# Loading K of a batch row in one transfer with 32 KB runs in an attention decode kernel

## The chip, the cores and the metric

The kernel runs on one core of one Trainium2 chip. The core has TensorE (PE: matrix multiplies and transposes, reading SBUF and writing PSUM), VectorE (DVE), ScalarE (ACT), GpSimd (POOL), the queue engine SyncE (SP), and 16 DMA engines that move data between HBM and the on-chip memory SBUF. The metric is device time in microseconds for one execution. Three runs of the kernel before took 194.97, 195.15 and 195.17 us; their median is 195.15 us.

## The reference: what is computed

One decode step (one token) for a batch of 8 with a model width of 512. Attention uses 32 query heads over 8 groups of K and V heads, head size 128, and only the last 2048 of 8192 cached positions. Then follows an MLP block, whose token-shift branch is zero for one token.

```
q = layernorm(x) @ wq                       # 8 x (32 heads x 128)
k, v = last 2048 positions of the caches    # per row: 8 groups x 2048 x 128, bf16
p = softmax(q . k / sqrt(128))              # 4 heads share a group
h = x + (p . v) @ wo
x1 = layernorm(h)                           # the MLP's first branch adds nothing
out = h + x1 + gelu(layernorm(x1) @ w3) @ w4
```

K and V are 4 MB each per batch row, 64 MB in all; the weights are another 12 MB.

## The kernel before, in words

Work is cut into 16 units, n = 0 to 15: unit n is batch row b = n // 2 and half t = n % 2 of the groups (four groups, `J`). One K load brings one unit, 2 MB: `load_k` (line 484) puts 32 partitions per group (`RR`) into SBUF, each with 64 consecutive positions, which is one contiguous run of 16 KB in HBM. `knat` has four such buffers (`NK`), and `vnat` four more for V. All large loads are issued on SP, in program order: SP waits for the buffer to be free, issues, and goes on to the next, so what stands behind a waiting issue waits too.

One unit is one step of the main loop, and it has four blocks (`U`). For each block `turn_K` transposes the block on TensorE as 8 matmuls of 32-bit pairs (line 313) into one of two PSUM buffers, the first half of which ScalarE copies out (line 300) and the second half VectorE (line 301), into one of the four `kT_sb` buffers (`NKT`). `pe_QK` (line 328) multiplies two blocks with the queries, 8 matmuls of 512 columns; it is called after the third and after the fourth block of a step. Scores of a row collect in one PSUM bank, 128 partitions (four groups by 32) by 512 columns.

After the second step of a row the softmax follows: maximum (`softmax_1`, line 338), its transposition and spreading (lines 342 to 356), `exp` into `P_sb` (line 359). In the next row's steps the probabilities are spread over groups on VectorE (`softmax_spread`, line 374, four parts), transposed (`softmax_4`, line 385) and multiplied with V three steps behind K (`pe_PV`, line 428, in the last three units line 418; four steps behind for the last two units). `fold`, `turn_o` and the lines 447 to 481 bring the result into the layout for the output weights.

The order on each engine is the order of the calls in the main loop. SP's order is: query weights, K 0, K 1, K 2, K 3, V 0, K 4, V 1, and so on in turns, the first half of the output weights (`load_wo`, line 494) after V 4, K 14 and K 15 together, V 11 to V 15, the second half of the output weights, then w3 and w4 into the K buffers (lines 626 on). A K load waits for the last turn of the unit that used its buffer, four units before; a V load waits for the product of V four units before. At the end come the product with the output weights (line 516), the layer norms, w3 (line 666) and w4 (line 700).

## Time and profile before

| | us |
|---|---|
| median of 3 runs | 195.15 |
| profiled execution | 195.02 |
| its span in the trace | 193.7 |
| PE busy | 142.1 |
| DVE busy | 107.6 |
| ACT busy | 89.5 |

The queue of SP moves 79.18 MB; its packets fill 96.7% of the 16 DMA engines' span, and the mean rate is 410 GB/s. The profile cuts the span into 40 equal slices of 4.84 us and gives for each the busy share of every engine and the clock granted to TensorE in tenths (9 is 90% or more), and the rate of the transfers in GB/s. The chain of waits is followed back from the last instruction, at each step to what released it. Timeline rows give the start in us, the length in us, engine and line, operation, output and inputs, the number of instructions merged, and in brackets how long the engine was idle before and what ended that. A wait of TensorE that was ended by the DMA of `knat` dates the arrival of a K load.

### The profile page before, as it was taken

Reading aid. Unit: us, or ns where it says so; the run is one execution under the profiler, and the core shown is the slowest. Engines: PE = TensorE matmul, PEld = TensorE weight load, DVE = VectorE, ACT = ScalarE, POOL = GpSimd, SP = SyncE. Lnnn points to the kernel's source line nnn. Section 1 sums busy time; section 2 is a strip of 40 time slices with the busy share of each in tenths; the row PEclk is TensorE's granted clock in tenths of the full one; section 3 lists DMA queues with packets and bytes.
Section 4 is the critical chain, followed back from the end, with each engine's and each line's share of the span. In section 5 each row is a group of like instructions: output and inputs, shape, how many; then the busy total and the mean of one; then the engine's idle time right before and its main releaser. Section 6 shows DMA issues by size and latency. Waiting matters only on the chain.

```text
span 193.7 us, 4489 instructions
## 1 busy us (share of the span) xinstructions
PE 142.1 (73%) x1972; PEld 110.8 (57%) x1972; DVE 107.6 (56%) x281; ACT 89.5 (46%) x115; POOL 7.8 (4%) x29
## 2 busy tenths in 40 slices
PE   0038895897999888708987867886497897797674
PEld 0037673574776647408675736564494664696672
DVE  5502544965777686602966565657155975753241
ACT  6000766764856646414464725482354754250041
POOL 5001001001000100100001000100000000000000
PEclk9999999999999999975999999999979999755555
DMA  6999999999999999999999999999999999999981
GB/s 225 433 430 430 430 430 433 426 430 431 423 423 416 426 425 426 426 430 423 430 433 426 430 420 433 423 421 433 430 426 423 423 430 426 430 423 415 409 351 58
DMA packets 5954, 79.46 MB, mean 410 GB/s; under 512 B 672, under 2 KB 688, under 8 KB 1456
## 3 DMA queue, kind: packets, MB, share of 16 engines
q1 hardware_dynamic: 5920, 79.18, 96.7%
q8 instruction: 15, 0.25, 0.5%
q14 instruction: 3, 0.02, 0.0%
q10 hardware_dynamic: 16, 0.01, 0.0%
HBM read 79.18 MB, written 0.01 MB: 409 GB/s over the span
## 4 chain that ended last, share of the span: by engine, by line
DMA 57%; PE 26%; DVE 12%; SPq 1%; issue 1%; ACT 0%
DMA knat<-in_A_k_cache_dram 45%; PE kT_ps L313 16%; DMA knat<-in_B_w_dram 12%; DVE kT_sb L301 6%; PE S_ps L328 5%; DVE Pz L374 3%; PE kT_ps L385 3%; DVE mcol L338 1%; SPq L204 1%; PE sm L447 1%; DVE Mrow L344 1%; PE sm L342 1%; PE S_ps L700 1%; PE sm L393 1%; DVE negrow L349 0%
## 5 line engine op out<-in xcount | busy, mean ns | idle before, releaser
L300 ACT ACTIVATE kT_sb<-kT_ps 128x1024 bf16<-128x1024 bf16 x64 | 62.5, 1025 | 42.8 <-PE kT_ps L313 42.8
L313 PE MATMUL kT_ps<-perm_k,knat 128*128 128x128 f32 x512 | 68.0, 288 | 13.8 <-DMA knat<-in_A_k_cache_dram 13.4
L313 PEld LDWEIGHTS kT_ps<-perm_k,knat 128*128 128x128 f32 x512 | 59.9, 148 | 21.6 <-DMA knat<-in_A_k_cache_dram 15.4
L301 DVE TENSOR_SCALAR kT_sb<-kT_ps 128x512 int32<-128x512 int32 x64 | 43.6, 689 | 38.5 <-PE kT_ps L313 38.5
L328 PE MATMUL S_ps<-kT_sb,qz 128*32 128x512 bf16 x256 | 19.8, 383 | 5.9 <-DVE kT_sb L301 3.9
L374 DVE TENSOR_TENSOR Pz<-P_sb,mJ 128x256 bf16<-128x256 bf16 x64 | 23.9, 418 | 0.0
L438 ACT ACTIVATE oE<-oT_ps 128x256 f32<-128x256 f32 x13 | 5.0, 385 | 28.5 <-PE oT_ps L428 28.5
L428 PE MATMUL oT_ps<-vnat,pS 128*32 128x256 bf16 x416 | 17.5, 275 | 0.9 <-DMA vnat<-in_A_v_cache_dram 0.9
L300 ACT ACTIVATE pS<-kT_ps 128x1024 bf16<-128x1024 bf16 x8 | 8.2, 1025 | 10.2 <-PE kT_ps L385 10.2
L428 PEld LDWEIGHTS oT_ps<-vnat,pS 128*32 128x32 bf16 x416 | 9.1, 96 | 3.9 <-DMA vnat<-in_A_v_cache_dram 1.0
L328 PEld LDWEIGHTS S_ps<-kT_sb,qz 128*32 128x32 bf16 x256 | 4.6, 94 | 10.8 <-ACT kT_sb L300 9.7
L301 DVE TENSOR_SCALAR pS<-kT_ps 128x512 int32<-128x512 int32 x8 | 5.5, 692 | 7.4 <-PE kT_ps L385 7.4
L385 PE MATMUL kT_ps<-perm_p,Pz 128*128 128x128 f32 x64 | 9.6, 298 | 0.0
L285 POOL COPY qz<-q_sb 64x64 bf16<-64x64 bf16 x16 | 4.7, 294 | 117.3 <-PE S_ps L328 101.5
L385 PEld LDWEIGHTS kT_ps<-perm_p,Pz 128*128 128x128 f32 x64 | 7.6, 151 | 3.0 <-issue 3.0
L267 PE MATMUL S_ps<-xlnT,wbig 128*128 128x8 bf16 x128 | 3.6, 168 | 7.6 <-DMA wbig<-in_A_wq_dram 7.6
L338 DVE TENSOR_REDUCE mcol<-S_ps 128x1 f32<-128x512 f32 x8 | 5.5, 692 | 4.5 <-PE S_ps L328 4.5
L447 PEld LDWEIGHTS sm<-selo,oE 128*128 128x128 f32 x52 | 7.7, 212 | 0.4 <-ACT oE L438 0.4
L447 PE MATMUL sm<-selo,oE 128*128 128x16 f32 x52 | 7.6, 261 | 0.3 <-DVE negcol L356 0.3
L267 PEld LDWEIGHTS S_ps<-xlnT,wbig 128*128 128x128 bf16 x128 | 3.5, 104 | 7.7 <-issue 7.7
L359 ACT ACTIVATE P_sb<-S_ps,negcol 128x512 bf16<-128x512 f32 x8 | 5.5, 688 | 3.8 <-DVE negcol L356 3.8
L459 DVE TENSOR_TENSOR oK<-o,mK 128x256 bf16<-128x256 f32 x16 | 6.8, 425 | 0.5
(96 smaller groups left out, 94.9 us busy)
## 6 DMA issues: line engine op xcount, KB each, us to landing
knat<-in_A_k_cache_dram SPq DMA_DIRECT2D x16, 2048.0 KB, 30.4
vnat<-in_A_v_cache_dram SPq DMA_DIRECT2D x16, 2048.0 KB, 34.7
wbig<-in_A_wq_dram SPq DMA_DIRECT2D x1, 4096.0 KB, 12.2
wbig<-in_A_wo_dram SPq DMA_DIRECT2D x2, 2048.0 KB, 26.0
knat<-in_B_w_dram SPq DMA_DIRECT2D x2, 896.0 KB, 19.7
knat<-in_B_w_dram SPq DMA_DIRECT2D x3, 512.0 KB, 22.1
knat<-in_B_w_dram SPq DMA_DIRECT2D x1, 256.0 KB, 23.0
x_sb<-in_A_x_dram ACTq DMA_DIRECT2D x1, 8.0 KB
```

The costliest lines, as they stand in the source:

```text
L267: ins = e.matmul(S_ps[0][:, h * B:(h + 1) * B], wq_v[:, kc, h * DH:(h + 1) * DH], xlnT[:, kc * B:(kc + 1) * B], start=(kc == 0), stop=(kc ...
L300: e_lo.append(AC.op(lambda e: e.activation(dst[:, 0:1024], ps[:, 0:1024], ACT.Copy), e_Tlo[k], *free))
L301: e_hi.append(DV.op(lambda e: e.tensor_single_scalar(dst[:, 1024:2048].bitcast(dt.int32), ps[:, 1024:2048].bitcast(dt.int32), 0, ALU.bitwi ...
L313: ins = e.matmul(ps[:, c * 128:(c + 1) * 128], src[:, c * 128:(c + 1) * 128], perm_k[:, :], is_transpose=True)
L328: ins = e.matmul(S_ps[b % 2][32 * j:32 * (j + 1), :].rearrange("p (c r) -> p c r", c=16), qz[:, b % 2, J * t + j, k, lo:lo + 32], kT[:, j, k],
L338: e_max[b] = DV.op(lambda e: e.tensor_reduce(mcol[:, :], S_ps[b % 2][:, :], AX.X, ALU.max), e_QK[4 * b + 3], e_mT.get(b - 1))
L359: e_exp[b] = AC.op(lambda e: e.activation(P_sb[:, :], S_ps[s][:, :], ACT.Exp, bias=negcol[:, s:s + 1], scale=1.0, accum_out=lcol[:, s:s + 1]),
L374: e_Pz[b, part] = DV.op(lambda e, o=o, p_bc=p_bc, m_bc=m_bc: e.tensor_tensor(Pz[:, 0, J * o:J * (o + 64)].rearrange("p (x j k) -> p x j k" ...
L385: ins = e.matmul(ps[:, c * 128:(c + 1) * 128], src[:, c * 128:(c + 1) * 128], perm_p[:, :], is_transpose=True)
L428: ins = e.matmul(oT_ps[MO * q:MO * (q + 1), NO * (n % 2):NO * (n % 2 + 1)], pS[:, b % 2, o:o + 2 * MO - 1:2], vnat[:, n % NV, (16 * w + 2 ...
L447: ins = e.matmul(sm[:, 32:48], oE[:, o:o + 128], selo[:, 16 * s:16 * s + 16], start=(s == 0), stop=(s == 2 * VP - 1))
L459: e_sc[n] = DV.op(lambda e: e.tensor_tensor(oK[:, n % 2], h_bc, k_bc, ALU.mult), e, e_mK, e_turn.get(n - 2))
```

## The change

K of a whole batch row is loaded by one DMA of 4 MB: 16 partitions for each of all 8 groups (`RK`), and each partition holds 128 consecutive positions, a run of 32 KB. The four `knat` buffers become two pairs, one pair per row. A load of a row now waits for the last turn of the row two before. Row 7 is the exception: its K is loaded by four DMAs of 1 MB with runs of 8 KB, two for each of its two units, and each unit has its own semaphore.

A step still turns four blocks, but each block now holds positions of all 8 groups. The permutation that orders the partitions of a turned block is for 8 groups of 16. The scores of a step are one call after its four blocks: 16 matmuls of 512 columns, for both halves of the groups. Columns of a score row therefore stand for other positions than before, and `exp` stores them with a step of two so that `P_sb` has the order of before, and everything behind it (spread, transposition, V) stays as it is. K loads are issued in the first step of a row, and the loads of w3 and w4 wait for the last turn of row 6.

```
-        sem_k = [S(f"sem_k{i}") for i in range(NK)]
+        sem_k = [S(f"sem_k{i}") for i in range(2)]
+        sem_kx = S("sem_kx")
...
+        def kpair(b):
+            return knat[:, 2 * (b % 2):2 * (b % 2) + 2, :].rearrange("p s f -> p (s f)")
+
         def turn_K(i):
-            n, u = divmod(i, U)
-            src = knat[:, n % NK, 2048 * u:2048 * (u + 1)].bitcast(dt.float32)
+            n, q = divmod(i, U)
+            b, x = divmod(n, NU)
+            u = 4 * (q // 2) + 2 * x + q % 2
+            src = kpair(b)[:, 2048 * u:2048 * (u + 1)].bitcast(dt.float32)
...
-            e_T[i], e_ev[i] = turn(mm, kT_sb[:, i % NKT, :], ((sem_k[n % NK], 16 * (n // NK + 1)),),
-                                   free=(e_QK.get((i - NKT) // 2),))
+            landed = (sem_kx, 32) if n == NUN - 1 else (sem_k[b % 2], 16 * (b // 2 + 1 + (n == NUN - 2)))
+            e_T[i], e_ev[i] = turn(mm, kT_sb[:, q, :], (landed,), free=(e_QK.get(n - 1),))
...
+        def pe_QK(n):
+            b, x = divmod(n, NU)
+            kT = kT_sb[:, :, :].rearrange("p u (c j r k) -> p j k (u c) r", c=8, j=G, k=2)
             def f(e):
-                for k in range(2):
-                    for j in range(J):
...
+                for t in range(NU):
+                    lo = 24 - 16 * t - 8 * x
+                    for k in range(2):
+                        for j in range(J):
+                            ins = e.matmul(S_ps[b % 2][32 * j:32 * (j + 1), :].rearrange("p (c r) -> p c r", r=RK),
+                                           qz[:, b % 2, J * t + j, k, lo:lo + 32], kT[:, J * t + j, k],
+                                           start=(t == 0 and x == 0 and k == 0),
+                                           stop=(t == NU - 1 and x == 1 and k == 1),
+                                           tile_position=(0, 32 * j), skip_group_check=True)
...
-            e_exp[b] = AC.op(lambda e: e.activation(P_sb[:, :], S_ps[s][:, :], ACT.Exp, bias=negcol[:, s:s + 1],
+            e_exp[b] = AC.op(lambda e: e.activation(P_sb[:, :].rearrange("p (c r v) -> p v c r", r=RK, v=2),
+                                                    S_ps[s][:, :].rearrange("p (v c r) -> p v c r", r=RK, v=2), ACT.Exp, bias=negcol[:, s:s + 1],
...
-        def load_k(n):
-            b, t = divmod(n, NU)
-            dma(SP, knat[:, n % NK, :],
-                A_k_cache[b, J * t:J * (t + 1), W0:SK, :].rearrange("j (r c) d -> r j (c d)", r=RR), sem_k[n % NK],
-                e_T.get(U * (n - NK + 1) - 1))
+        def load_k(b):
+            free = e_T.get(2 * U * (b - 1) - 1)
+            src = A_k_cache[b, :, W0:SK, :]
+            if b < NB - 1:
+                dma(SP, kpair(b), src.rearrange("j (r c) d -> r j (c d)", r=RK), sem_k[b % 2], free)
+            else:
+                src = src.rearrange("j (r v x c) d -> r j v x (c d)", r=RK, v=2, x=2)
+                dst = kpair(b).rearrange("p (v x f) -> p v x f", v=2, x=2)
+                for x, sem in ((0, sem_k[b % 2]), (1, sem_kx)):
+                    for v in range(2):
+                        dma(SP, dst[:, v, x, :], src[:, :, v, x, :], sem, free)
...
         for n in range(NUN):
-            if n < NUN - 1:
-                load_k(n)
-            if n == NUN - 2:
-                load_k(n + 1)
+            if n % NU == 0:
+                load_k(n // NU)
...
-            pe_QK(2 * n)
             if t == 1 and b >= 1:
                 softmax_4(b - 1)
             turn_K(i + 3)
...
-            pe_QK(2 * n + 1)
+            pe_QK(n)
...
-                e_T[U * (NUN - NK + 1) - 1])
+                e_T[2 * U * (NB - 1) - 1])
```

More of the change, by code (lines that the diff above doesn't have):

```diff
@@ L32 @@
 RR = 32
+RK = 16
 NCU = W // RR
@@ L245, in bass_sequential_preLN__sliding_block_cached__mixer_s_mlp__decode_kernel @@
                     ap=[ident_f[:, :].ap[0], [0, 2], [2, 64]]))) for k in range(2)]
-        e_pk = DV.op(lambda e: e.tensor_copy(perm_k[:, :].rearrange("p (j r) -> p j r", j=J),
-                                             ident_f[:, :].rearrange("p (r j) -> p j r", j=J)))
+        e_pk = DV.op(lambda e: e.tensor_copy(perm_k[:, :].rearrange("p (j r) -> p j r", j=G),
+                                             ident_f[:, :].rearrange("p (r j) -> p j r", j=G)))
         e_pp = DV.op(lambda e: e.tensor_copy(perm_p[:, :].rearrange("p (x j h) -> p x j h", j=J, h=R),
@@ L287, in fill_q @@
                     q_sb[64 * c:64 * (c + 1), :, :, b].rearrange("p k (g h) -> p g k h", h=R)),
-                    e_qs, (PO.sem, PO.count), e_QK.get(2 * (NU * (b - 2) + 1) + 1))
+                    e_qs, (PO.sem, PO.count), e_QK.get(NU * (b - 2) + 1))
         e_T, e_Tlo, e_Thi, e_lo, e_hi, e_QK, e_PV = {}, [], [], [], [], {}, {}
@@ L315, in mm @@
                 return ins
-            e_T[i], e_ev[i] = turn(mm, kT_sb[:, i % NKT, :], ((sem_k[n % NK], 16 * (n // NK + 1)),),
-                                   free=(e_QK.get((i - NKT) // 2),))
-        def pe_QK(m):
-            n, v = divmod(m, 2)
-            b, t = divmod(n, NU)
-            lo = 24 - 16 * t - 8 * v
-            kT = kT_sb[:, (2 * m) % NKT:(2 * m) % NKT + 2, :].rearrange("p u (c j r k) -> p j k (u c) r", c=8, j=J, k=2)
-            def f(e):
-                for k in range(2):
-                    for j in range(J):
-                        ins = e.matmul(S_ps[b % 2][32 * j:32 * (j + 1), :].rearrange("p (c r) -> p c r", c=16),
-                                       qz[:, b % 2, J * t + j, k, lo:lo + 32], kT[:, j, k],
-                                       start=(t == 0 and v == 0 and k == 0), stop=(t == NU - 1 and v == 1 and k == 1),
-                                       tile_position=(0, 32 * j), skip_group_check=True)
+            landed = (sem_kx, 32) if n == NUN - 1 else (sem_k[b % 2], 16 * (b // 2 + 1 + (n == NUN - 2)))
[3 more added lines that the diff above has]
+            kT = kT_sb[:, :, :].rearrange("p u (c j r k) -> p j k (u c) r", c=8, j=G, k=2)
+            def f(e):
+                for t in range(NU):
[7 more added lines that the diff above has]
+                                           tile_position=(0, 32 * j), skip_group_check=True)
                 return ins
-            e_QK[m] = PE.op(f, *e_ev[2 * m], *e_ev[2 * m + 1], e_qw[b], e_qs, e_exp.get(b - 2))
+            e_QK[n] = PE.op(f, *(e for q in range(U) for e in e_ev[U * n + q]), e_qw[b], e_qs, e_exp.get(b - 2))
         sm_read = [e_xT]
@@ L338, in softmax_1 @@
             e_max[b] = DV.op(lambda e: e.tensor_reduce(mcol[:, :], S_ps[b % 2][:, :], AX.X, ALU.max),
-                             e_QK[4 * b + 3], e_mT.get(b - 1))
+                             e_QK[NU * b + 1], e_mT.get(b - 1))
         def softmax_2(b):
@@ L482, in turn_o @@
             e_scale[n] = DV.op(g, e)
-        def load_k(n):
-            b, t = divmod(n, NU)
-            dma(SP, knat[:, n % NK, :],
-                A_k_cache[b, J * t:J * (t + 1), W0:SK, :].rearrange("j (r c) d -> r j (c d)", r=RR), sem_k[n % NK],
-                e_T.get(U * (n - NK + 1) - 1))
+        def load_k(b):
[9 more added lines that the diff above has]
+                        dma(SP, dst[:, v, x, :], src[:, :, v, x, :], sem, free)
         def load_v(n):
@@ L633, in bass_sequential_preLN__sliding_block_cached__mixer_s_mlp__decode_kernel @@
             dma(SP, w4_sb[:, 4 * a:4 * a + 4, :].rearrange("p c n -> p (c n)"), w4_a[:, a, :], sem,
-                e_T[U * (NUN - NK + 2) - 1])
+                e_T[2 * U * (NB - 1) - 1])
         dma(SP, w4_sb[:, FA:FC, :].rearrange("p c n -> p (c n)"),
```

## The prediction

> **What bounds the kernel now.** I read the forty slices first, then the chain of waits, then windows and the timeline around two places: K's arrivals late in the run, and the tail.

> ```profile
> PEclk9999999999999999975999999999979999755555
> DMA  6999999999999999999999999999999999999981
> DMA packets 5954, 79.46 MB, mean 410 GB/s; under 512 B 672, under 2 KB 688, under 8 KB 1456
> q1 hardware_dynamic: 5920, 79.18, 96.7%
> DMA 57%; PE 26%; DVE 12%; SPq 1%; issue 1%; ACT 0%
> ```

> The DMA row is full in 37 of 40 slices: one queue moves 79.18 MB without a pause, and TensorE (142.1 of 193.7 us busy) waits for it. The packet count says how runs become packets: 42 DMAs close with 16 small packets each (the 672), and the other 5,248 are one per contiguous run; the query weights have 128 runs of 32 KB and count 128, so 32 KB is one packet too. The chain ends on that queue:

> ```profile
> 61.39 36.20 DMA knat<-in_A_k_cache_dram
> ...
> 103.42 34.90 DMA knat<-in_A_k_cache_dram
> ...
> 167.59 22.88 DMA knat<-in_B_w_dram
> 190.47 0.04 issue
> 190.51 0.62 PE S_ps L700 x16
> ```

> A 2 MB load "takes" 35 us because it stands in the queue. Now the timeline (start, length, engine, idle before, who ended it):

> ```profile
> 87.85 4.81 PE L313 MATMUL kT_ps<-perm_k,knat 128*128 128x128 f32 x24 [5.53 <-DMA knat<-in_A_k_cache_dram]
> 107.45 2.86 PE L313 MATMUL kT_ps<-perm_k,knat 128*128 128x128 f32 x24 [0.66 <-DMA knat<-in_A_k_cache_dram]
> 117.23 2.86 PE L313 MATMUL kT_ps<-perm_k,knat 128*128 128x128 f32 x24 [2.21 <-DMA knat<-in_A_k_cache_dram]
> 133.46 0.62 PE L428 MATMUL oT_ps<-vnat,pS 128*32 128x256 bf16 x16 [0.85 <-DMA vnat<-in_A_v_cache_dram]
> 138.36 4.13 PE L313 MATMUL kT_ps<-perm_k,knat 128*128 128x128 f32 x24 [2.96 <-DMA knat<-in_A_k_cache_dram]
> ```

> K arrivals are 9.8 us apart (107.45, 117.23, 127.02), one K and one V of 2.1 MB each: 429 GB/s. Then V arrives at 133.4, 6.4 us after K where 4.9 is usual, and everything up to the output weights stays 1.5 us late, while the GB/s row shows no dip: the bytes flow, but the slowest of the 16 engines slipped, and a load has landed only when the slowest has. Also, after 5.5 us of idleness 24 turns take 4.81 us, after 2.96 us 4.13, after 2.21 us 2.86. The tail:

> ```profile
> 181.15 0.23 DVE L481 TENSOR_REDUCE o<-oM 128x16 bf16<-128x64 bf16 x1
> 182.51 1.85 PE L516 MATMUL S_ps<-o,wbig 128*128 128x8 bf16 x64 [1.68 <-DMA wbig<-in_A_wo_dram]
> 189.38 2.17 PE L700 MATMUL S_ps<-knat,Pz 128*32 128x128 bf16 x56 [0.26 <-DMA knat<-in_B_w_dram]
> ```

> Here the compute is close behind the transfers: from the last row's softmax (164.97) TensorE and VectorE work almost without a gap to 181.38, 1.1 us before the output weights land; the last layer waits 0.3 us for its weights. The profiled execution took 195.02 us (span 193.7 and 1.3 around it), 0.13 below the median of 195.15.

> **The change part by part.**
> *Packets.*

> ```profile
> 5.00:12.50 7.50, 0.29 (x4) 0.20 (x4) 2.65 (x12) 0.00 (x0) 0.00 (x0) 1.00 1.00 433
> 20.00:32.00 12.00, 9.36 (x89) 6.57 (x87) 6.13 (x10) 8.15 (x9) 0.59 (x2) 1.00 1.01 433
> ```

> (Windows; the last three columns are granted clock, DMA share, GB/s.) Seven rows of K go from 16 to 8 packets per engine. The 16 KB stream runs at 429 GB/s by its arrivals; the 32 KB load of the query weights ran at 433 (window 5 to 12.5 us). For 4.19 MB that is 9.78 against 9.69, so 0.09 us a row and 0.65 us in all, or 12 ns a packet. But the K window from 20 to 32 us also shows 433 with 16 KB runs, which prices a packet at nothing. Row 7 goes the other way: four DMAs with 8 KB runs, 16 more packets per engine, up to 0.19 us. Five DMAs fewer save 5 closing packets per engine, at most 0.06. Net: between 0 and -0.5 us; I take -0.4, nearer to the arrivals, which time whole loads, than to a window with cut edges.

> *Start.* K of row 0 lands whole, 4.85 us later than its first half did (17.79 to 22.65). This delays TensorE only, if the queue stays full. It holds the query weights, 4 MB, 4 MB and 2 MB of V, and V lands at 22.65 + 9.7 + 4.9 = 37.2. The next issue, K of row 2, must wait for all eight turns of row 0, and SP holds every V behind it. Query weights issued at 0.73 landed at 12.95 with 9.7 us of data: an issue needs 2.5 us ahead, so K must be issued by 34.7. Row 0's turns took from 17.84 to 29.36; without the score block between them they end at 22.65 + 11.0 = 33.7, or 34.2 if the first 24 run at 4.81 instead of 4.00. Issued at 34.25 at the latest: margin 0.5 us, cost nothing. If the margin is gone, the shortfall goes straight into the end. Row 1's turns end near 50 against 54; later margins exceed 10 us.

> *Scores.* 16 score matmuls at the end of a step for 8 and 8: same count, columns and stride (383 ns a record, 0.62 us per 8). In the first step of a row (107.45) VectorE sets the pace: its fourth eviction ends 5.9 us after the start, the first 8 matmuls were hidden before that, now all 16 follow: +0.6 us a row. In the second step the gap that the earlier block leaves is filled by turns, paced by the 1.025 us evictions of ScalarE: about 0. Evictions write the four blocks that the scores have just read; the scores precede those turns on TensorE, so no new wait, and behind the scores stand only V's products and the softmax's matmuls, counted in the row. A row is then 17.4 us warm (7.6 + 0.6 + 9.2) against 19.6 between arrivals: hidden, 2.2 us to spare.

> *Exp.* Same 512 columns, stored with a step of two: 0.69 us now; no row shows that step on this store, so between 0 and a doubling, of which one in eight lies in the tail. I take 0, as the turns' evictions and the score reads with the same step cost their element count. *Spread, permutation copy, w3/w4's other wait* (turn 55 instead of 51, past by 150 us; both are queued behind V at 164.5): 0. Row 7's four K issues take SP 4 x 0.54 instead of 2 x 0.54 us; they go out near 127 and V behind them is needed near 141: 0. POOL's query copies wait for the same scores, with a row to spare.

> *The last rows.* K of row 6 is now one load and ends where V ended before: 133.4 if the slip of 1.5 us falls ahead of it again, 131.9 if not. Row 6 takes 17.4, row 7 16.6 (15.95 measured, + 0.6), so the last softmax is through at 165.5 to 167.0 instead of 164.97. The tail takes 0.1 (V at 172.75) + 1.1 (output weights) + 0.3 (last layer) = 1.5 us of such lateness before the end moves. I take the slip to fall later: it came while TensorE was in row 6's first step, which now starts only when that K has landed. Then the lateness is about 0.5, covered.

> Sum: 195.15 - 0.4 = 194.7 (from the profiled run 194.6).

> [...] The K loads of before already read four groups that lie 2 MB apart, at 429 GB/s; eight such groups are the same distance. [...]

> **The rivals.**
> *The tail overtakes the transfers (slower).* If the slip falls before K of row 6, TensorE idles from 129.4 (row 5: 112.0 + 17.4) to 133.0: 3.6 us, longer than the 2.96 that cost 1.45 us at 138.36 (10.64 against 9.2 for the step). Row 6 ends at 152, row 7 at 168.5: 3.5 us late, 1.5 covered: 195.0 + 2.0 = 197.0. It decides from 1.5 us of lateness on; warm it is 2.0, and 195.6. For it: 3 us gaps do go cold here. Against: the slip may move. [...]
> *The queue runs dry* before K of row 2: a slow first row of TensorE, up to 1.5 us past the margin, 195.0 to 196.2.
> *Eight groups read slower*: at the 400 GB/s that the trace shows at worst while the queue is full (182.5 to 185 us) seven rows take 73.4 instead of 68.4 us: 199.7. The step from four groups to eight is what no row here shows.
> *Packets cost nothing:* 195.1, the change does nothing to the time.

> **How the numbers follow.** Forecast 194.2 to 194.95 around 194.7, chance 0.44: 0.36 of it faster by over 0.2% (below 194.76; 0.2% is about what a measurement of this kernel can tell), 0.08 within. Packets at nothing 0.14, all within. Tail 0.29: slower 0.27, within 0.02. Dry queue 0.07: slower. Slow groups 0.06: slower. Faster 0.36, same 0.24, slower 0.40. Range 194.2 to 197.1: it takes in the tail and the dry queue, and leaves out the slow groups and half of a tenth at each end.

> **What would show it.** DMA row full in the slices around 34 to 38 us, and the third K issue before 34.7; K arrivals one per row, 19.5 us apart; 5,200 packets on the queue (5,248 - 7 x 128 + 256 = 4,608, and 37 x 16 = 592 small); the last softmax before 166.5 and the wait for the output weights still there. Wrong if that wait is gone, if a slice near 36 us is not full, or if K's arrivals are further apart than 19.6 us.

## The result and the profile after

The changed kernel takes 296.0 us (median of 6 runs, 286.78 to 310.77) where the kernel before takes 195.1: 1.479 times as long, 95% interval 1.469 to 1.489. The ratio comes from the three shortest of seven runs (286.78, 288.01 and 290.86 us, the last not among the six); the profiled one took 302.55 us, so what follows splits a difference of 107.5 us between spans, where for the shortest run it is 91.7.

The slices and packets of the changed kernel:

```profile
DMA  8999998999899989999999999998999999619960
GB/s 323 374 207 209 209 209 176 366 205 212 259 400 200 218 257 429 330 211 211 287 370 209 207 252 394 200 226 238 372 219 222 239 329 362 255 67 389 409 282 20
q1 hardware_dynamic: 5200, 79.18, 93.2%
```

The 16 DMA engines are nearly as busy as before (packets fill 93.2% of their span, 96.7% before), the bytes are the same, and the packets are the 5,200 of the forecast. But sixteen slices carry 200 to 226 GB/s instead of 425, and those at 360 to 430 are the ones in which mostly the query weights, V or the weights behind it pass. The kept trace has the start, length and size of every packet: one of 32 KB takes 1.21 us (the median) for the query weights and 2.54 us for K. Three arrivals of K on TensorE's timeline and a window in which the queue holds nothing but K:

```profile
113.05 4.84 PE L320 MATMUL kT_ps<-perm_k,knat 128*128 128x128 f32 x24 [13.01 <-DMA knat<-in_A_k_cache_dram]
150.46 4.91 PE L320 MATMUL kT_ps<-perm_k,knat 128*128 128x128 f32 x24 [18.97 <-DMA knat<-in_A_k_cache_dram]
184.29 5.06 PE L320 MATMUL kT_ps<-perm_k,knat 128*128 128x128 f32 x24 [15.39 <-DMA knat<-in_A_k_cache_dram]
```
```profile
14.00:31.00 17.00, 3.59 (x114) 3.02 (x111) 1.12 (x2) 0.00 (x0) 1.16 (x4) 1.00 1.03 213
```

From the fourth row on, rows of K arrive 34 to 37 us apart where the forecast had 19.5 (the first four are 20.2, 26.8 and 31.7 us apart), and TensorE stands idle for 13 to 19 us before each of the three shown. At 210 GB/s the 4.19 MB of a row take 20.0 us instead of 9.8: 82 us over eight rows, of 107.5 us between the two spans. Some 10 us are lost near 265 us, when the queue is nearly empty:

```profile
264.00:267.00 3.00, 3.00 (x31) 2.79 (x33) 2.37 (x4) 2.98 (x4) 0.00 (x0) 1.00 0.19 82
```

There the last V load stands in SP's order before all remaining weights and waits for a product of row 5, which TensorE reaches only after the late K of row 7. (From 258 to 273 us the rates are 287, 109, 82, 55 and 180 GB/s in steps of 3 us; against 430 that is 10 us.) The packet records split the whole: per engine, K's packets take some 80 us more than at their usual length, those of V and the weights some 14 us more than before, and the time without a packet is some 14 us longer, 10 of them near 265 us.

### The profile page after: what moved, and what is told of

Same layout as the page of the kernel before. It is cut to its first block, busy times and chain, and to the rows that moved or that the text cites. A ratio compares the mean times of both kernels' runs of the same rounds, so it can differ in the third digit from the quotient of the medians.

```text
span 301.2 us, 4468 instructions
## 1 busy us (share of the span) xinstructions
PE 151.5 (50%) x1972; PEld 125.3 (42%) x1972; DVE 107.5 (36%) x281; ACT 91.5 (30%) x115; POOL 7.7 (3%) x29
## 2 busy tenths in 40 slices
DMA packets 5234, 79.46 MB, mean 264 GB/s; under 512 B 592, under 2 KB 608, under 8 KB 1376
## 3 DMA queue, kind: packets, MB, share of 16 engines
q1 hardware_dynamic: 5200, 79.18, 93.2%
HBM read 79.18 MB, written 0.01 MB: 263 GB/s over the span
## 4 chain that ended last, share of the span: by engine, by line
DMA 34%; PE 30%; another core or an unknown queue 23%; DVE 9%; ACT 2%; issue 1%; SPq 1%
DMA knat<-in_A_k_cache_dram 26%; PE kT_ps L320 18%; DMA knat<-in_B_w_dram 8%; PE S_ps L335 5%; DVE kT_sb L303 3%; DVE Pz L383 2%; PE oT_ps L437 2%; PE kT_ps L394 2%; DVE mcol L346 1%; ACT kT_sb L302 1%; SPq L206 1%; PE sm L402 1%; DVE oK L468 1%; DVE Mrow L352 1%
## 5 line engine op out<-in xcount | busy, mean ns | idle before, releaser
L320 PE MATMUL kT_ps<-perm_k,knat 128*128 128x128 f32 x512 | 79.5, 323 | 103.0 <-DMA knat<-in_A_k_cache_dram 103.0
L320 PEld LDWEIGHTS kT_ps<-perm_k,knat 128*128 128x128 f32 x512 | 73.6, 172 | 106.1 <-DMA knat<-in_A_k_cache_dram 104.2
L302 ACT ACTIVATE kT_sb<-kT_ps 128x1024 bf16<-128x1024 bf16 x64 | 63.7, 1024 | 139.4 <-PE kT_ps L320 139.3
L335 PE MATMUL S_ps<-kT_sb,qz 128*32 128x512 bf16 x256 | 17.7, 395 | 4.7 <-ACT kT_sb L302 2.1
L335 PEld LDWEIGHTS S_ps<-kT_sb,qz 128*32 128x32 bf16 x256 | 6.5, 97 | 11.4 <-ACT kT_sb L302 6.2
L287 POOL COPY qz<-q_sb 64x64 bf16<-64x64 bf16 x16 | 4.6, 290 | 195.4 <-PE S_ps L335 179.2
L367 ACT ACTIVATE P_sb<-S_ps,negcol 128x512 bf16<-128x512 f32 x8 | 6.6, 828 | 4.2 <-DVE negcol L364 4.2
L477 PE MATMUL sm<-oK,mE 128*32 128x64 bf16 x64 | 3.5, 211 | 6.6 <-DVE oK L468 6.6
```

What stands on the lines that cost most here:

```text
L302: e_lo.append(AC.op(lambda e: e.activation(dst[:, 0:1024], ps[:, 0:1024], ACT.Copy), e_Tlo[k], *free))
L320: ins = e.matmul(ps[:, c * 128:(c + 1) * 128], src[:, c * 128:(c + 1) * 128], perm_k[:, :], is_transpose=True)
L335: ins = e.matmul(S_ps[b % 2][32 * j:32 * (j + 1), :].rearrange("p (c r) -> p c r", r=RK), qz[:, b % 2, J * t + j, k, lo:lo + 32], kT[:, J ...
L367: e_exp[b] = AC.op(lambda e: e.activation(P_sb[:, :].rearrange("p (c r v) -> p v c r", r=RK, v=2), S_ps[s][:, :].rearrange("p (v c r) -> p ...
```

## The experiments

The question is which property of the new load halves its rate. Three theories: A, the distance of the eight groups in HBM; B, the run of 32 KB; C, the way in which a load of 16 x 8 partitions (outer times inner dimension of the source) is shared out among engines.

### Loads alone, eleven forms

A kernel that only loads K: each phase loads 8.4 MB and SP waits until it has landed, so that the times of the issues are the times of the phases. Source and partitions of a load, with sizes in KB:

```
 1: [32 x 16 KB][4 groups, 2 MB apart], run 16      2: [16 x 32 KB][8 groups, 2 MB], run 32
 3: [32 x 32 KB][4 groups, 2 MB], run 32            4: [16 x 32 KB][8 groups, 2 MB], run 16
 5: [16 x 16 KB][8 groups, 2 MB], run 16            6: as 2, groups 2 MB - 4 KB apart
 7: as 2, groups 2 MB - 32 KB apart                 8: as 2, groups 2 MB - 128 KB apart
 9: [128 x 32 KB], run 32                          10: [64 x 32 KB][2 groups, 2 MB], run 32
11: as 2, other rows
```

> This kernel only loads K, in eleven phases, and waits for each phase before the next; nothing of the layer is computed, x is returned. Each phase moves 8 MB. After (shares of the transfer in the changed kernel: 207 GB/s while K streams, 430 while V does) the question is which property of the new load halves the rate. Theory A, distance: eight groups 2 MB apart on the 16 engines make engines meet in the same part of HBM. Then the phases with eight groups exactly 2 MB apart (2, 4, 5, 11) run near 207 GB/s, four groups (1, 3), two groups (10) and a contiguous stretch (9) near 430, and moving the groups 32 or 128 KB closer (7, 8) brings most of it back. Theory B, run length: 32 KB runs are slow from the cache. Then 2, 3, 6 to 8, 10 and 11 are near 207 and 4 and 5, with 16 KB, near 430. Theory C, the split of the work over engines by 16 partitions per group: then everything with eight groups (2, 4 to 8, 11) is slow whatever the distance.

The issues on SP, one row per phase (start in us, time on the queue engine, loads):

```profile
0.73 2.64 SPq L38 DMA_DIRECT2D ka<-in_A_k_cache_dram  x4
23.05 1.22 SPq L38 DMA_DIRECT2D kb<-in_A_k_cache_dram  x2
65.56 1.21 SPq L38 DMA_DIRECT2D ka<-in_A_k_cache_dram  x2
87.65 2.53 SPq L38 DMA_DIRECT2D kb<-in_A_k_cache_dram  x4
129.49 2.52 SPq L38 DMA_DIRECT2D ka<-in_A_k_cache_dram  x4
170.73 1.18 SPq L38 DMA_DIRECT2D kb<-in_A_k_cache_dram  x2
213.45 1.18 SPq L38 DMA_DIRECT2D ka<-in_A_k_cache_dram  x2
255.80 1.18 SPq L38 DMA_DIRECT2D kb<-in_A_k_cache_dram  x2
298.17 0.84 SPq L38 DMA_DIRECT2D ka<-in_A_k_cache_dram  x2
320.01 1.22 SPq L38 DMA_DIRECT2D kb<-in_A_k_cache_dram  x2
```

The difference between two starts is a phase. Form 1 took 22.3 us, form 2 42.5, form 3 22.1, form 4 41.8, and forms 9 and 10 21.8 and 22.2. Forms 1 and 3 differ in the run, 16 or 32 KB, and in the number of loads, and by 0.2 us. Everything with 16 x 8 partitions takes twice the time, with 16 or 32 KB runs (B falls) and with the groups moved closer by 4, 32 or 128 KB (6: 42.7, 7: 42.4, 8: 42.4; A falls).

### The load alone, in the old kernel and undone in the new one

In the kernel before, K of a step now comes from eight groups:

```
-                A_k_cache[b, J * t:J * (t + 1), W0:SK, :].rearrange("j (r c) d -> r j (c d)", r=RR), sem_k[n % NK],
+                A_k_cache[b, :, W0 + 1024 * t:W0 + 1024 * (t + 1), :].rearrange("j (r c) d -> r j (c d)", r=16), sem_k[n % NK],
```

> The kernel before, in which each K load of 2 MB reads 1024 positions of all eight groups, 16 partitions each in runs of 16 KB, instead of 2048 positions of four groups; the scores are therefore those of a mixed order and the output is not the layer's. Sizes, number of loads, buffers and all compute stay. Theory A and theory C: K streams at about 207 GB/s, so 16 x 2.1 MB take 162 instead of 78 us, and the time is about 275 to 290 us. Theory B: 195 us, as 16 KB runs are the old ones. A theory that puts the loss on the 4 MB loads or on the new order of scores: 195 us.

Two runs: 285.1 and 329.4 us, one in the expected range of A and C and one above it. And in the changed kernel, K comes from four groups:

```
-            src = A_k_cache[b, :, W0:SK, :]
+            src = A_k_cache[b, 0:4, SK - 4096:SK, :]
...
-                dma(SP, kpair(b), src.rearrange("j (r c) d -> r j (c d)", r=RK), sem_k[b % 2], free)
+                dma(SP, kpair(b), src.rearrange("j (r c) d -> r j (c d)", r=32), sem_k[b % 2], free)
```

> The changed kernel, in which K of a row is read from 4096 positions of four groups (32 partitions each, runs of 32 KB; 8 KB for row 7) instead of 2048 positions of eight groups; everything else of the change stays, and the output is not the layer's. Theory A and C: full rate again, and the time is that of the rest of the change: by my forecast's terms 194.7 us, or up to 197 if the tail overtakes the transfers. Theory B: still near 290 us. If the loss sits in the buffers or in the order of the scores: also near 290 us.

197.0 us (195.37 to 199.91), 1.010 of the kernel before (1.006 to 1.013). So the source pattern of the K load makes the difference in both directions; 4 MB loads, row buffers and the order of the scores are together worth 1%.

### Which part of the sharing

> Loads of K alone again, in eleven phases; nothing of the layer is computed. Theory A (distance of the groups) has fallen: groups 4, 32 or 128 KB closer still took 42.4 us for 8 MB. New theory D, ports of SBUF: with 16 as the outer dimension of the load each of the 16 engines gets one outer index, that is eight neighbouring partitions; with 32 x 4 it gets four partitions and the four that lie 32 further. If these two fours share a way into SBUF, then in the first case always two engines stand at the same one. Rival C2: the source, eight separate streams, is what is slow. Phase 2 (16 x 8 out of one stretch of HBM) and 4 (16 x 8, each run read eight times, little of HBM): D 42 us both, C2 22. Phases 3 and 5 (the same with 32 x 4): 22 by both. Phases 6 to 8 (loads into 64, 32 and 16 partitions, 4, 2 and 1 MB): by D 64 and 32 partitions have the same eight ways, and 16 have four, so 22, 12 and 12 us; if only the engines count, 12, 7.5 and 5. Phases 9 to 11 put a full load ahead and then shift engines by loads in which only 12, 8 and 4 engines take part: by D, 9 (engines 0 to 3 and 8 to 11 half a cycle off their partners) takes about 10 + 15 + 20 + 2.5 = 47 us, 10 (all alike) 10 + 19 + 39 + 2.5 = 70, and 11 (only engines 0 to 3 shifted) 10 + 39 + 2.5 = 52, its rate falling to a quarter in the last third. By C2 the last loads keep 39 us in 9 too: 60 us or more.

```
 2: [16 x 288 KB][8 x 32 KB]     3: [32 x 144 KB][4 x 32 KB]     one stretch of HBM
 4: [16 x 32 KB][8 x 0]          5: [32 x 32 KB][4 x 0]          each run read again
 6, 7, 8: [64], [32], [16 x 32 KB] into partitions 0 to 63, 0 to 31, 0 to 15, two loads each
```

```profile
22.83 1.21 SPq L38 DMA_DIRECT2D kb<-in_A_k_cache_dram  x2
66.15 1.21 SPq L38 DMA_DIRECT2D ka<-in_A_k_cache_dram  x2
88.66 1.21 SPq L38 DMA_DIRECT2D kb<-in_A_k_cache_dram  x2
131.00 1.21 SPq L38 DMA_DIRECT2D ka<-in_A_k_cache_dram  x2
153.18 1.15 SPq L38 DMA_DIRECT2D kb<-in_A_k_cache_dram  x2
176.10 0.81 SPq L38 DMA_DIRECT2D ka<-in_A_k_cache_dram  x2
188.42 0.78 SPq L38 DMA_DIRECT2D kb<-in_A_k_cache_dram  x2
199.70 2.80 SPq L38 DMA_DIRECT2D kb<-in_A_k_cache_dram  x4
```

The last phases were meant to shift engines against each other by half a cycle, that is by four of the eight runs that an engine has in a load. They took 62.5, 72.6 and 60.3 us for 47, 70 and 52: the first and the third are misses. In the first, the load that held 12 engines back filled partitions 0 to 47, where by theory D's map engines 0 to 3 and 8 to 11 meet. In the third only engines 0 to 3 were shifted. By the theory engines 0 to 7 should then have run at full rate, but the whole stays at half rate:

```profile
366.00:376.00 10.00, 0.00 (x0) 1.00 0.98 210
```

The third expectation below, 60 us, repeats what was measured here, so meeting it says nothing. A second try:

```
-            for k, p in ((12, 0), (8, 64), (4, 96)):
+            for k, p in ((12, 32), (8, 96), (4, 0)):
```

> Three phases of K loads, repeating the shifting phases, since the first try was flawed: the load that held back 12 engines filled partitions 0 to 47, where engines 0 to 3 and 8 to 11 meet by the theory's own map (partitions p and p + 32), so the shift of half a cycle (4 runs of 32 KB, 4.9 us) came out as a whole one. Now the holding loads fill partitions 32 to 79, 96 to 127 and 0 to 15, in which no two engines meet. Theory D (ports): phase 1, a full load, 12 + 8 + 4 engines held back by four runs, then two loads of the changed kernel's form, 9.7 + 14.6 + 19.4 + 2.5 = 46 us, with about 430 GB/s over the stretch in which all engines work. Phase 2, all held back alike: 71 us as before (72.6). Phase 3, only engines 0 to 3 shifted: engines 0 to 7 at full rate, 8 to 15 at half, 320 GB/s and later 108, 60 us as before. Rival C2 (the source, or anything that does not depend on which engines coincide): phase 1 takes 62 us or more.

61.6, 72.2 and 60.1 us: the first phase missed again. Two of its windows tell more than its length:

```profile
37.00:42.00 5.00, 0.00 (x0) 1.00 0.88 210
42.00:47.00 5.00, 0.00 (x0) 1.00 0.95 393
```

By the packet records every engine first has packets of 1.21 us (the full load), then twelve of some 2.5 us, and from about 43 us on mostly 1.21 us again. By then all 16 engines load K in the changed kernel's own form, 16 x 8 partitions; the first are through at 47 us. In the second phase, with all held back alike, packets stay at some 2.5 us to the end. So a shift by half a cycle, as the theory has it, does bring the full rate in this form (393 GB/s); what failed were the holding loads, which ran at half rate themselves. By the map, while 8 engines still held, the other 8 were already at K and at the same half of the ports.

In the third phase, while engines 0 to 3 hold, the map puts three engines at some ports: there the packets of all 16 engines take some 3.65 us, and then 2.5 us on all of them, the first eight included (the expected 320 GB/s did not come). If the map holds, one crowded port slows all 16 engines; neither that nor why is shown. A trace does not name the engine of a packet either: the records are put in chains by their times, and which partitions an engine fills is taken from the theory, which these times fit.

The whole changed kernel with these loads ahead:

```
         dma(SP, wq_v, A_wq.rearrange("(p k) n -> p k n", k=KC), sem_wq)
...
+        for k, p in ((12, 32), (8, 96), (4, 0)):
+            dma(SP, vpair[p:p + 4 * k, :], bass.AP(tensor=hold.tensor, offset=hold.offset,
+                                                   ap=[[73728, k], [16384, 4], [1, 16384]]), sem_hold)
```

> The changed kernel, and behind the query weights three more loads of data that nobody uses (3 MB): 12, then 8, then 4 engines get four runs of 32 KB each, into V buffers that are still free. They put engines 0 to 3 and 8 to 11 half a cycle off the engines with which theory D has them share a port. K, scores and all else are those of the changed kernel. Theory D: K streams at up to 430 GB/s; the end moves by the 12 useless runs of engines 0 to 3, 14.6 us: 195 to 197 + 14.6 = 210 us, up to 230 if the shift is partly lost on the way, against 287 to 311 for the changed kernel. Any theory in which the source, the run length, the buffers or the order of the scores costs the time: 287 us or more, as 3 MB are added and nothing is taken away.

335.8 us (326.99 to 338.55), longer than without, and over 100 us above the expected time. Here too the window from 42 to 47 us has 367 GB/s after 210, but from 47 us on, once V passes, it falls to 282 and 190.

### A shift that meets nobody

K of a row as two loads: groups 0 to 3 into partitions 0 to 63, groups 4 to 7 into 64 to 127. By the theory an engine then has four neighbouring partitions in each, engines e and e + 8 lie 32 partitions apart, and one load of 8 engines, in phase 2 only, puts half of them half a cycle behind.

```
+            yield from lead(t)
+            yield o[64:96, 1, :], ap(6, 0, 0, [[144 * KB, 8], [32 * KB, 4], [1, 16384]])
+            yield from halves((2, 3))(t)
```

> Three phases of K loads, a cleaner trial of the shift. In the last one the holding loads themselves met other engines at the ports, by the theory's map, so nothing could be told. Here K of a row is two loads: groups 0 to 3 into partitions 0 to 63, groups 4 to 7 into 64 to 127, 16 x 4 partitions with runs of 32 KB; an engine then has four neighbouring partitions in each, and engines e and e + 8 (partitions 32 apart) meet. Phase 1, a full load and two rows so: theory D (ports) 9.7 + 39 + 2.5 = 51 us. Phase 2, engines 0 to 7 held back by four runs into partitions 64 to 95, which no other engine uses at that time: from then on engines 0 to 7 and 8 to 15 are always in different halves, so D says full rate, 9.7 + 4.9 + 19.4 + 2.5 = 36.5 us, shorter than phase 1 with 1 MB more to load. Phase 3, all 16 held back by four runs into partitions 0 to 63: 9.7 + 9.7 + 39 + 2.5 = 61 us. Rival E (an engine is slow at partitions that are not its usual ones, whoever else is there): phase 2 takes phase 1's time and up to 5 us more, 51 to 56 us.

The starts of the three phases and of what follows, then a window of phase 1 and one of phase 2 (the last columns are clock, DMA share and GB/s):

```profile
0.73 0.40 SPq L38 DMA_DIRECT2D kb<-in_A_k_cache_dram  x1
...
53.19 1.20 SPq L38 DMA_DIRECT2D ka<-in_A_k_cache_dram  x2
...
91.14 0.93 SPq L38 DMA_DIRECT2D kb<-in_A_k_cache_dram  x2
...
153.23 0.31 SPq L96 DMA_DIRECT2D x_sb<-in_A_x_dram  x1
```
```profile
32.00:37.00 5.00, 0.00 (x0) 1.00 1.07 223
...
67.00:72.00 5.00, 0.00 (x0) 1.00 1.05 419
```

52.5, 38.0 and 62.1 us for 51, 36.5 and 61. The same loads, with 1 MB more ahead of them, take 14.5 us less, at 419 GB/s instead of about 210; by the theory because half of the engines come later. Source pattern, runs and partitions are the same in phases 1 and 2 (only the rows differ), and a load of twice as many runs ahead, which by the theory holds all 16 engines back alike, phase 3, brings nothing (62.1 us, 190 to 236 GB/s). So the same loads run at either rate, depending on what went ahead, as collisions at the ports have it (rival E falls).

In the whole kernel, first without and then with the holding load:

```
-                dma(SP, kpair(b), src.rearrange("j (r c) d -> r j (c d)", r=RK), sem_k[b % 2], free)
+                for h in range(2):
+                    dma(SP, kpair(b)[64 * h:64 * h + 64, :], src[J * h:J * h + J].rearrange("j (r c) d -> r j (c d)", r=RK),
+                        sem_k[b % 2], free)
...
```

> The changed kernel with K of a row as two loads of four groups into 64 partitions each (runs of 32 KB, 8 KB in row 7; the permutation of the turns follows). The layer is computed in full. Theory D and rival E: half rate as in the changed kernel, 280 to 310 us. If eight groups in one load were the cause: 195 to 198 us.

279.2 and 294.8 us: half rate, though no load has eight groups any more.

```
+        dma(SP, vnat[64:96, 2:4, :].rearrange("p s f -> p (s f)"),
+            bass.AP(tensor=hold.tensor, offset=hold.offset, ap=[[73728, 8], [16384, 4], [1, 16384]]), sem_hold)
...
```

> The kernel with two loads per row, and behind the query weights one more load of 1 MB of data that nobody uses, in which only engines 0 to 7 take part, four runs of 32 KB each. Theory D: K at full rate, 195.4 to 197 us of the four-group version + 4.9 = 200 to 203 us; more, up to 240, if the half cycle of 4.9 us is partly lost to instruction loads on the way. Rival E: as without the extra load or slower, 280 to 310 us.

299.5 us (298.7 to 301.56): the expected time is missed by nearly 100 us, its upper bound by 60. Its windows show where the rate is lost:

```profile
17.00:22.00 5.00, 0.92 (x14) 0.35 (x11) 1.12 (x2) 0.00 (x0) 1.16 (x4) 1.00 1.03 416
...
37.00:42.00 5.00, 4.52 (x48) 3.66 (x40) 2.52 (x4) 3.56 (x4) 0.00 (x0) 1.00 1.00 210
```

K of row 0 and more than half of row 1 flows at about 416 GB/s (193 in the same window without the holding load) and row 0 arrives at 29.5 instead of 34.2 us, although 4.9 us of useless data go ahead. From about 32 us on, when the first V load begins, the rate is back at 210. By the theory every engine has a port of its own in a V load, but engines that are half a cycle apart are in V and in K at the same time. The packet records agree: from 32 us on V's packets of 16 KB take 1.2 to 1.3 us where 0.61 is usual, and K's take 2.5. That engines in V meet engines in K at the ports is still argued, not shown.

### The rest of the change

> The kernel before, in which both score blocks of a step stand at its end, where the changed kernel has them. My forecast's term: hidden, 0 us in 195.1; up to +0.6 us per row where VectorE sets the pace, which the tail covers up to 1.5 us. A theory that the order of the scores is what keeps the four-group version of the change at 195.4 to 197.6 us expects 196 to 197.

```
-            pe_QK(2 * n)
             if t == 1 and b >= 1:
...
+            pe_QK(2 * n)
             pe_QK(2 * n + 1)
```

195.05 us, ratio 0.9996 (0.9987 to 1.0005): the order of the scores is free.

> The kernel before, in which both K loads of a row are issued together when the row two before is through, and the turns of a row wait for both (the last row apart); runs, partitions and scores stay. If the buffers by whole rows (later start, third load issued with no margin) are what keeps the four-group version above 195.1, this takes 195.5 to 197 us; by my forecast's term 195.1.

```
...
-                e_T.get(U * (n - NK + 1) - 1))
+                e_T.get(2 * U * (b - 1) - 1))
...
-            if n < NUN - 1:
+            if n % NU == 0:
                 load_k(n)
-            if n == NUN - 2:
                 load_k(n + 1)
```

196.99 us, ratio 1.0138 (1.0069 to 1.0207), as expected if the loads by rows cost the time. The third row of K is issued at 36.76 us, and a window of 1 us shows the queue running dry:

```profile
37.00:38.00 1.00, 0.39 (x8) 0.15 (x8) 0.46 (x1) 0.98 (x2) 0.00 (x0) 1.00 0.04 16
```

The four-group version has the same gap (issue at 34.96, 49 GB/s in that window). With a V load ahead of the third K:

```
+            if n == LVD + 1:
+                load_v(1)
             if n % NU == 0:
                 load_k(n // NU)
...
```

> The four-group version of the changed kernel (K of a row from 4096 positions of four groups, so not the layer's scores), in which the second V load is issued ahead of the third K load instead of behind it. That load waits for nothing, so the queue holds 2 MB, 4.9 us, more when SP stands before the third K. Theory F (the 1% that the four-group version and the kernel with loads by rows lose is the queue running dry near 37 us, which their windows show as 49 and 16 GB/s in one slice of 1 us): the gap is gone and the time is 194.4 to 195.3 us, which would be my forecast for all of the change but the rate of K. If the 1% lies in the scores or the tail: 196 to 197.5 as before.

196.12 us (194.73 to 197.2), ratio 1.0039 (1.0014 to 1.0063): 1.0 us above before, 0.8 above the expected range. It lies in the range expected if the scores or the tail cost the 1%, and the scores cost nothing by the run above. Three of the twelve runs took 194.73 to 194.95 us, the time of the forecast, which runs of the kernel before reach too (from 194.81). The gap is gone (475 GB/s from 38 to 39 us). What is late in the profiled run of 196.42 us is the last two rows:

```profile
132.79 5.38 PE L320 MATMUL kT_ps<-perm_k,knat 128*128 128x128 f32 x24 [3.94 <-DMA knat<-in_A_k_cache_dram]
...
184.33 0.23 DVE L490 TENSOR_REDUCE o<-oM 128x16 bf16<-128x64 bf16 x1
```

K of row 6 finds TensorE idle for 3.94 us, its first 24 turns take 5.38 us, the last softmax is through at 167.25 instead of 164.97, and the row's output is ready at 184.56 instead of 181.38, behind the output weights.

## Why the prediction was wrong

**The packets: the term that failed.** The forecast took the rate of the 32 KB runs from the query weights and from the old K loads, and found 0 to 0.5 us to gain. A run's length was the wrong property to read off: the weights have 128 partitions in one dimension and the old K 32 x 4, while the new load has 16 x 8. That division halves the rate, whatever the run and the source (42.5 us against 22.1 for 8.4 MB). The account that fits the times is theory D's, an account of ports that no run shows directly: with 16 outer indices each of 16 engines fills eight neighbouring partitions, two ports, and always two engines stand at the same port; half a cycle apart they run at full rate (419 GB/s in that trial). K takes 20.0 us a row for 9.69. The term was -0.4 us and came to some +82 (80 by the packet records). The price of the run itself may have been right: forms 1 and 3 differ by 0.2 us for 8.4 MB, in one run, where the forecast had 0.09 us for 4.19 MB.

**The rival that came nearest was priced at a twentieth.** "Eight groups read slower" had a chance of 0.06 and took its price, 5 us, from the slowest full window, 400 GB/s, as no row showed eight groups. The measured rate was 210, and the end moved by 101 us. The distance of the groups in HBM, which the prediction weighed, was the wrong thing to look at: it is about the source, and the source did not matter (42.4 to 42.7 us with the groups moved closer, 42.5 without).

**The start was off in its sign.** The margin before the third K was forecast as 0.5 us, with the issue at 34.25 at the latest. At full rate the issue came at 34.96 (four groups) and 36.76 (loads by rows), and 34.7 was needed. In both, K of row 0 arrived later than the forecast 22.65, at 23.92 and 24.05 us; the four-group version's turns then took the forecast 11.0 us. So the queue does run dry, up to some 2 us, and the dry-queue rival, with 0.07, was priced too low. What the gap costs the four-group version is open: its profiled run has the gap and took 195.37 us, the others 196.43 to 199.91.

**The scores were right:** 0 forecast, 0.9996 measured. **Exp:** 0 forecast, 0.69 us now 0.83, a small miss.

**The tail rival's mechanism occurs:** lateness from 1.5 us on decides, forecast 195.6 to 197.0; with the gap closed, the four-group version's profiled run (196.42 us) has 2.3 us of it, a first step of row 6 whose first 24 turns take 5.38 us after 3.94 us of idleness, and no wait left for the output weights. One trace shows this, and not every run was that long.

At full rate the change took 197.0 us, and 196.1 with V ahead, inside the stated range and not faster. So nothing here points to a version that beats the kernel before.

## What to carry to other kernels

How a load is divided into outer and inner dimension can halve its rate: here 16 x 8 partitions took 42.5 us for 8.4 MB and 32 x 4 took 22.1. That two engines then stand at one port of SBUF is the author's account, which fits the times and is not shown. Busy DMA engines don't show the loss (93.2% of the span after, 96.7% before); GB/s (about 210 against 425) and the length of a 32 KB packet (2.54 against 1.21 us) do. Before changing the partition split of a load, look for a load in the trace with the same split (outer and inner count), not one with the same run or size. Where a load's rate is the bound of a kernel, time the new form alone first: a kernel of a few loads with a wait between them gives it in 20 to 45 us per form.

## What the runs showed of the hardware

- 16 x 8 partitions load at about 210 GB/s (42.5 us for 8.4 MB), 32 x 4, 64 x 2 and 128 at about 425 (21.8 to 22.3 us); for 16 x 8 and 32 x 4 whatever the source, even with each run read eight or four times.
- 64 partitions (0 to 63) load no faster than 32 (206 and 214 GB/s), 16 at 119.
- The half rate depends on time: with one load of 32 runs ahead (by the theory eight engines, four runs each) the same loads ran at 419 GB/s instead of about 210, and 16 x 8 loads went from 210 to 393 GB/s in the first phase of the second try, by the theory when a shift of half a cycle came about.
- A packet of 32 KB takes 1.21 us at full rate, about 2.5 us in loads at half rate (two engines at a port by the map), and about 3.65 in the third phase of the second try, while engines 0 to 3 hold (three at some ports by the map); there the packets of all 16 engines lengthen together, also of those that the map has at free ports.
- The DMA share stays at 0.9 to 1.1 at half rate, since the packets fill the time by taking twice as long (2.54 us for 1.21).
